# Output projections of 128 columns per column tile, all heads summed in PSUM, token rows copied by GpSimd, new part orders

## The chip, the cores and the metric

The kernel runs on one core of one Trainium2 chip. A core has TensorE (matrix multiplies into PSUM), VectorE, ScalarE and GpSimd (elementwise work; GpSimd here only on SBUF), and SyncE, which issues most of the DMAs. Each runs its own stream of instructions; semaphores tie them together. The metric is the device time in microseconds of one execution, median of three runs.

## The reference

The reference is one transformer layer on 2048 tokens of width 512. Part A is attention in 64 segments of 32 tokens with a recurrent memory of 8 rows: each segment attends, with 32 heads of 128, over 8 memory rows and its own 32 rows, and the first 8 rows of its output become the memory of the next segment. Part B is an MLP of width 1792 over all tokens. Cut to what matters:

```python
for s in range(n_seg):                       # 64 segments of 32 tokens
    xs = x[:, s * seg_len:(s + 1) * seg_len, :]
    h = jnp.concatenate([mem, xs], axis=1)   # 8 + 32 rows
    q, k, v = (jnp.einsum('btd,dhe->bhte', h, W) for W in (Wq, Wk, Wv))
    scores = jnp.where(mask, jnp.einsum('bhqe,bhke->bhqk', q, k) * scale, -1e9)
    o = jnp.einsum('bhqk,bhke->bhqe', softmax(scores), v)
    o = jnp.einsum('bhte,hed->btd', o, Wo)   # the output projection, sum over 32 heads
    mem = o[:, :M, :]
    outs.append(o[:, M:, :])
h = x + concatenate(outs)                    # x went in normalised
h2 = h + mlp(layernorm(h))                   # second norm inside mlp
```

## The kernel before

**Tiling.** A segment's tokens are split: 24 of its rows (`NA`) are packed with the 8 memory rows into one group of 32 (pack A), and the remaining 8 rows of four segments form another group of 32 (pack B). 32 columns are one column tile of TensorE, so most matmuls carry 32 columns of weights and four of them run side by side, at `tile_position` (0, 32 j). Each such matmul is issued with a weight load of its own. Where two steps in a row use the same activations as weights, the second drops its four loads (`matmul_kept`, line 547).

**A segment** (the loop over `s`, from line 1303) is a set of named parts. K0, K1, Q0, Q1, V0, V1 are passes of four units each (`passes`, matmuls on line 796, 512 columns of weights moving): a unit is four loads and four matmuls. SC0 and SC1 are scores (line 963), PV0, PV1 and PVA apply the probabilities to V (lines 994, 998, 1055), SA are the scores of the 24 + 8 rows (line 1025). F0 and F1 are passes of pack B for the next four segments in three segments out of four, and in the fourth one F1 is **WO_B** (`wo_B`), the output projection of pack B of the four segments before. **WO** (`wo`, `wo_units`) is the output projection of pack A, in eight units. Its result gives the memory rows of the next segment (tile hT) and 24 token rows of an earlier one (tile opT).

**WO before.** The heads are split into two halves by `a`, the 512 output columns into two halves by `b`; column tile j = 2a + b sums 16 heads into 256 columns of PSUM. Then VectorE transposes 128 x 256 (line 1095) into TT, and `halves_add` (line 1089) adds the two halves of heads, in two instructions for hT and two for opT. **WO_B before:** column tile j sums 8 heads into all 512 columns (line 1112); ScalarE copies half of it (line 1118), VectorE adds twice (lines 1119, 1120) into oBn, 32 rows by 512.

**`nat`** (line 1122) turns four segments' opT by a DMA transpose into oN, writes oBn's rows into oN by four DMAs, adds oN to the residual xr and takes the statistics of the second norm.

**What sets the order.** TensorE's order is written out by hand: `ORDERS` has for each kind of segment (`a1` to `a3` the first ones, `m0` to `m3` by s mod 4, `z60` to `z63` the last) a list of part.from.to; `TURNED` tells which passes run their four units backwards. The other engines are put in order by a list scheduler (`Sched.schedule`): a cost for each operation, a rank by the longest way to the end, plus `BONUS`, a table of numbers by kind and place. `S.either` lets it choose between ScalarE and VectorE. `align` adds weight loads that do nothing (line 794) to the passes: `LEAD` = 199 of them in all early on, and with `LOCK` = 106 up to a full count of 256 (`FETCH_N`) instructions every four segments, so that every four segments begin at the same place modulo 256. What follows the last segment (from line 1478) is the second half of part B, with 128-row matmuls.

Of the kernel before, what the change touches and what calls it, by code (L numbers as in the profile page):

```python
# [21 lines left out]
TURN = 1.27  # L22
# [4 lines left out]
LOCK = 106  # L27
# [9 lines left out]
BONUS = {"": 3.88, "EC0": 19.37, "EC0@a1": -40, "EC0@a2": 0, "EC0@a3": 2.13, "EC0@m0": 4.48, "EC0@m1": 40, "EC0@m2": 0, "EC0@m3": -7.71,  # L37
# [527 lines left out]
def build_kernel(nc, A_x, A_mem0, A_Wq, A_Wk, A_Wv, A_Wo, B_w1, B_b1, B_w2, B_b2, out):  # L565
# [3 lines left out]
    with st:  # L569
# [132 lines left out]
        def load(fn, kb, writes):  # L702
            chain.append(S.dma(fn, kb, writes=writes))
# [896 lines left out]
```

## Time and profile before

| | |
|---|---|
| device time, three runs | 804.42, 807.74, 809.25 us |
| median | 807.74 us |
| span of the profiled execution | 802.2 us |
| granted TensorE clock, mean | 0.998 |
| ScalarE busy | 558.0 us |
| GpSimd busy | 90.1 us |
| DMA moved | 48.77 MB, mean 61 GB/s |

The profile is one execution; its times are compared with its own span, which is 5.5 us below the median of the runs. In groups of instructions a row reads: line, engine, operation, what is written from what, shape, count, busy us in all, mean ns of one, and after the bar the engine's idle time just ahead of them with what ended it. In windows, each engine has its busy us and in brackets its instructions in the stretch, then the granted clock, the DMA share and GB/s. PEld is TensorE's weight loads. "issue" is time in which an engine waited for nothing that the profile shows. q8 is one of the DMA queues, of kind "instruction". A line can be a helper's, as 796 and 814 are.

### The profile page before, as it was taken

Reading aid. Unit: us, or ns where it says so; the run is one execution under the profiler, and the core shown is the slowest. Engines: PE = TensorE matmul, PEld = TensorE weight load, DVE = VectorE, ACT = ScalarE, POOL = GpSimd, SP = SyncE. Lnnn points to the kernel's source line nnn. Section 1 sums busy time; section 2 is a strip of 40 time slices with the busy share of each in tenths; the row PEclk is TensorE's granted clock in tenths of the full one; section 3 lists DMA queues with packets and bytes.
Section 4 is the critical chain, followed back from the end, with each engine's and each line's share of the span. In section 5 each row is a group of like instructions: output and inputs, shape, how many; then the busy total and the mean of one; then the engine's idle time right before and its main releaser. Section 6 shows DMA issues by size and latency. Waiting matters only on the chain.

```text
span 802.2 us, 46835 instructions
## 1 busy us (share of the span) xinstructions
PE 775.9 (97%) x21699; PEld 423.1 (53%) x20880; DVE 600.7 (75%) x1847; ACT 558.0 (70%) x1580; POOL 90.1 (11%) x211
## 2 busy tenths in 40 slices
PE   2899999999999999999999999999999999999998
PEld 1455555555555555555555555555555555644444
DVE  3277878888888888888888888888888888732311
ACT  1557777777777777777778777777777777773342
POOL 5022000010001010101010101000000000020700
PEclk9999999999999999999999999999999999999999
DMA  9961010201111121102010202010212112074300
GB/s 367 394 174 24 4 37 11 45 12 37 26 33 30 30 33 27 36 19 42 19 43 15 49 12 50 13 37 20 50 25 56 51 38 59 17 232 127 86 27 26
DMA packets 65555, 48.77 MB, mean 61 GB/s; under 512 B 28996, under 2 KB 63308, under 8 KB 63820
## 3 DMA queue, kind: packets, MB, share of 16 engines
q1 hardware_dynamic: 65024, 45.50, 20.3%
q8 instruction: 166, 2.72, 1.4%
q14 instruction: 33, 0.27, 0.1%
q10 hardware_dynamic: 332, 0.27, 0.1%
HBM read 31.08 MB, written 8.13 MB: 49 GB/s over the span
## 4 chain that ended last, share of the span: by engine, by line
PE 91%; DMA 3%; DVE 2%; ACT 1%; SPq 1%; issue 1%; POOL 0%; DVEq 0%; ACTq 0%
PE ps L796 43%; PE ps L1083 15%; PE ps L547 8%; PE quad L1465 6%; PE ps L1451 5%; DMA WQ<-in_A_Wq_dram 3%; PE ps L1112 3%; PE quad L994 3%; PE quad L1055 2%; PE ps L1025 2%; PE ps L1233 1%; PE ps L963 1%; PE quad L963 1%; SPq L708 1%; PE quad L998 1%
## 5 line engine op out<-in xcount | busy, mean ns | idle before, releaser
L1083 PE MATMUL ps<-WO,OT 128*32 128x256 bf16 x4224 | 140.6, 274 | 0.1
L796 PE MATMUL ps<-WQ,hT 128*32 128x512 bf16 x1864 | 131.6, 379 | 0.7 <-DVE hT L1089 0.5
L796 PE MATMUL ps<-WV,hT 128*32 128x512 bf16 x1364 | 125.2, 381 | 0.0
L796 PE MATMUL ps<-WK,hT 128*32 128x512 bf16 x1700 | 123.6, 380 | 0.1
L815 ACT ACTIVATE kq<-ps 128x512 bf16<-128x512 f32 x160 | 95.4, 597 | 32.3 <-PE ps L796 26.4
L1083 PEld LDWEIGHTS ps<-WO,OT 128*32 128x32 bf16 x4224 | 100.9, 96 | 26.5 <-ACT OT L814 5.5
L814 ACT CAST kq<-ps 128x512 bf16<-128x512 f32 x162 | 94.8, 585 | 19.9 <-PE ps L796 13.1
L814 ACT CAST OT<-quad 128x128 bf16<-128x128 f32 x191 | 84.4, 442 | 27.0 <-PE quad L998 18.8
L839 DVE STREAM_TRANSPOSE KALL<-kq 128x256 f32<-128x256 f32 x160 | 71.2, 445 | 15.0 <-ACT kq L814 11.8
L796 PEld LDWEIGHTS ps<-WQ,hT 128*32 128x32 bf16 x1864 | 50.3, 97 | 58.8 <-issue 19.0
L861 POOL COPY ZC<-QTB 128x256 bf16<-128x256 bf16 x64 | 25.6, 401 | 477.2 <-PE ps L963 455.7
L796 PEld LDWEIGHTS ps<-WK,hT 128*32 128x32 bf16 x1700 | 45.8, 96 | 56.9 <-issue 14.5
L547 PE MATMUL ps<-WV,hT 128*32 128x512 bf16 x684 | 67.6, 379 | 0.0
L796 PEld LDWEIGHTS ps<-WV,hT 128*32 128x32 bf16 x1364 | 38.4, 97 | 47.3 <-issue 36.6
L839 DVE STREAM_TRANSPOSE QT<-kq 128x256 f32<-128x256 f32 x128 | 57.0, 445 | 6.5 <-ACT kq L815 1.9
L1454 ACT ACTIVATE WQ<-ps,b1t 128x512 bf16<-128x512 f32 x42 | 28.9, 688 | 46.6 <-PE ps L1451 46.6
L1095 DVE STREAM_TRANSPOSE TT<-ps 128x256 f32<-128x256 f32 x66 | 29.7, 450 | 36.3 <-PE ps L1083 36.1
L814 ACT CAST VS<-ps 128x512 bf16<-128x512 f32 x65 | 38.1, 586 | 26.6 <-PE ps L796 26.5
L814 DVE CAST VS<-ps 128x512 bf16<-128x512 f32 x63 | 41.8, 663 | 5.4 <-PE ps L796 5.4
L1541 DVE TENSOR_TENSOR WV<-quad,WV 128x512 bf16<-128x512 f32 (+1 forms) x16 | 10.5, 672 | 45.6 <-PE quad L1465 45.6
L982 DVE TENSOR_TENSOR PC<-EC,rsc 128x128 bf16<-128x128 f32 x128 | 39.7, 310 | 4.3
L1112 PE MATMUL ps<-WO,OTB 128*32 128x512 bf16 x512 | 42.1, 381 | 0.4 <-issue 0.2
(163 smaller groups left out, 1432.1 us busy)
## 6 DMA issues: line engine op xcount, KB each, us to landing
WV<-in_A_Wv_dram SPq DMA_DIRECT2D x4, 1024.0 KB, 8.5
WK<-in_A_Wk_dram SPq DMA_DIRECT2D x4, 1024.0 KB, 14.2
WQ<-in_A_Wq_dram SPq DMA_DIRECT2D x4, 1024.0 KB, 24.7
WO<-in_A_Wo_dram SPq DMA_DIRECT2D x8, 512.0 KB, 9.4
v_last<-VSB SPq DMA_DIRECT2D x60, 64.0 KB, 2.9
VBD<-v_last SPq DMA_DIRECT2D x60, 64.0 KB, 2.9
h_mid<-xr SPq DMA_DIRECT2D x16, 128.0 KB, 1.8
WK<-in_B_w_dram SPq DMA_DIRECT2D x4, 512.0 KB, 4.6
```

The source lines that it names most:

```text
L547: return e.add_instruction(mybir.InstMatmult(name="I-%d" % (4000000 + _kept[0]), engine=mybir.EngineType.PE, start_tensor_calc=start, stop ...
L796: ins = e.matmul(o, l, m, start=(k == 0), stop=(k == DC - 1), tile_position=(0, 32 * j), skip_group_check=True)
L814: return {"act": (lambda e: e.copy(out, src), t_act(n, ps_)), "dve": (lambda e: e.tensor_copy(out, src), 0.16 + 1.042e-3 * n * fast)}
L815: return {"act": (lambda e: e.mul(out, src, scale_), t_act(n, ps_)), "dve": (lambda e: e.tensor_scalar(out, src, scale_, None, ALU.mult), ...
L839: S.op("dve", lambda e: e.transpose(out, src), reads=[("kq", i)], writes=[key], dur=t_dve(256) + 0.02, after=after)
L982: S.op("dve", lambda e: e.tensor_tensor(PC[:, r].rearrange("p t a -> p a t"), EC[:, r], bc, ALU.mult), reads=[("EC", r), ("rsc", r)], writ ...
L1083: ins = e.matmul(ps[bank][32 * j:32 * j + 32, 0:256], lhs(slot(h)), wo_cols(h, b), start=(k == 0), stop=(k == 15), tile_position=(0, 32 * ...
L1095: S.op("dve", lambda e: e.transpose(tt.rearrange("p c q t -> p (c q t)"), ps[bank][:, 0:256]), reads=[("ps", bank)], writes=[("TT", par)], ...
L1112: ins = e.matmul(ps[bank][32 * j:32 * j + 32, :], OTB[:, bk % 2, slot(h), :], WO[:, h, :], start=(k == 0), stop=(k == 7), tile_position=(0 ...
L1451: ins = e.matmul(ps[bank][:, 0:SBT], W1[:, cc, fc * P:(fc + 1) * P], hnT_of(k)[:, cc, :], start=(cc == 0), stop=(cc == DC - 1))
L1454: S.op("act", lambda e: e.activation(gT[:, fc, :], ps[bank][:, 0:SBT], ACTF.Gelu_apprx_tanh, bias=b1t[:, fc:fc + 1], scale=1.0), reads=[(" ...
L1465: S.op("pe", lambda e: e.matmul(quad[:, t, :], lhs, W2[:, fc, :], **flags), reads=[("W2", part_of(fc))] + gT_keys(k, fc), writes=[("ps", t ...
```

## The change

WO gives each column tile 128 of the 512 output columns and lets it sum all 32 heads, so nothing is left to be added after it. VectorE's transpose is 128 x 128; the memory rows go to hT by one copy on ScalarE or VectorE, the token rows to opT by one copy on GpSimd. WO_B uses the same units on OTB; its transpose goes to TTB, and GpSimd copies it into the rows of opT that were zero before. So `nat` needs no oBn and no four DMAs, and the memset of opT goes. WO's weights are loaded in head order. `LOCK` is None. `ORDERS` and `BONUS` are new throughout; `TURNED`, the banks and everything else stay.

```diff
-LOCK = 106
+LOCK = None
...
-          "m0": "Q0.0.2 Q1.0.1 Q0.2.4 K0.0.4 Q1.1.4 K1.0.4 SC0.0.1 V0.0.1 V1.0.2 V0.1.2 V1.2.3 V0.2.4 SC1.0.1 V1.3.4 F0.0.1 PVA.0.2 PV0.0.1 F0.1.4 WO.0.2 PV1.0.1 WO.2.8 F1.0.4 SA.0.1",
-          "m1": "K0.0.1 Q0.0.2 K0.1.2 Q0.2.4 K0.2.3 Q1.0.1 K0.3.4 Q1.1.4 K1.0.4 SC0.0.1 V1.0.1 V0.0.2 V1.1.2 V0.2.3 V1.2.3 V0.3.4 SC1.0.1 V1.3.4 F0.0.1 PVA.0.2 PV0.0.1 F0.1.4 WO.0.2 PV1.0.1 WO.2.8 F1.0.3 SA.0.1 F1.3.4",
-          "m2": "K0.0.2 Q0.0.4 K0.2.4 Q1.0.4 K1.0.4 SC0.0.1 V1.0.1 V0.0.2 V1.1.2 V0.2.3 V1.2.3 V0.3.4 SC1.0.1 V1.3.4 F0.0.2 PVA.0.2 PV0.0.1 F0.2.4 WO.0.2 PV1.0.1 WO.2.8 SA.0.1 F1.0.4",
-          "m3": "K0.0.1 Q0.0.2 K0.1.2 Q0.2.4 K0.2.4 Q1.0.4 K1.0.4 SC0.0.1 V1.0.1 V0.0.1 V1.1.2 V0.1.3 V1.2.3 V0.3.4 SC1.0.1 F1.0.1 V1.3.4 PVA.0.2 PV0.0.1 F1.1.5 WO.0.1 PV1.0.1 WO.1.8 F1.5.7 SA.0.1 F1.7.8",
+          "m0": "Q0.0.4 K0.0.3 Q1.0.1 K0.3.4 Q1.1.4 K1.0.4 V0.0.1 SC0.0.1 V0.1.3 V1.0.1 V0.3.4 F0.0.1 V1.1.2 F0.1.2 SC1.0.1 V1.2.4 PVA.0.2 PV0.0.1 F1.0.1 F0.2.4 WO.0.2 PV1.0.1 WO.2.8 SA.0.1 F1.1.4",
+          "m1": "Q0.0.4 K0.0.1 K1.0.1 K0.1.4 Q1.0.4 K1.1.4 V1.0.1 SC0.0.1 V0.0.2 V1.1.2 V0.2.4 V1.2.3 SC1.0.1 F0.0.1 V1.3.4 F0.1.3 PVA.0.2 PV0.0.1 F1.0.1 F0.3.4 WO.0.1 PV1.0.1 WO.1.8 F1.1.3 SA.0.1 F1.3.4",
+          "m2": "K0.0.2 Q0.0.4 K0.2.4 K1.0.1 Q1.0.4 K1.1.4 V1.0.1 SC0.0.1 V0.0.4 V1.1.2 SC1.0.1 F0.0.1 V1.2.4 F0.1.2 PVA.0.2 PV0.0.1 F0.2.4 WO.0.1 PV1.0.1 WO.1.3 F1.0.1 WO.3.8 F1.1.2 SA.0.1 F1.2.4",
+          "m3": "Q0.0.4 K0.0.2 Q1.0.1 K1.0.1 K0.2.4 Q1.1.3 V1.0.1 Q1.3.4 K1.1.4 V1.1.2 SC0.0.1 V0.0.1 V1.2.3 V0.1.4 SC1.0.1 F1.0.2 V1.3.4 F1.2.3 PVA.0.2 PV0.0.1 F1.3.5 WO.0.2 PV1.0.1 WO.2.8 SA.0.1 F1.5.8",
...
-        def wo_cols(h, dh):
-            return WO[:, h, :].rearrange("p (b two e) -> p two b e", two=2, e=32)[:, dh]
+        def wo_cols(h, j):
+            return WO[:, h, :].rearrange("p (c g e) -> p g c e", g=4, e=32)[:, j]
...
                 def f(e, q=q):
-                    for k in (2 * q, 2 * q + 1):
-                        for a in range(2):
-
-                            h = (k // 8) * 16 + 8 * a + k % 8
-                            for b in range(2):
-                                j = 2 * a + b
-                                ins = e.matmul(ps[bank][32 * j:32 * j + 32, 0:256], lhs(slot(h)), wo_cols(h, b), start=(k == 0), stop=(k == 15),
-                                               tile_position=(0, 32 * j), skip_group_check=True)
+                    for h in range(4 * q, 4 * q + 4):
+                        for j in range(4):
+                            ins = e.matmul(ps[bank][32 * j:32 * j + 32, 0:P], lhs(slot(h)), wo_cols(h, j), start=(h == 0), stop=(h == H - 1),
+                                           tile_position=(0, 32 * j), skip_group_check=True)
                     return ins
...
-            S.op("dve", lambda e: e.transpose(tt.rearrange("p c q t -> p (c q t)"), ps[bank][:, 0:256]), reads=[("ps", bank)], writes=[("TT", par)], dur=t_dve(256) + 0.02)
+            S.op("dve", lambda e: e.transpose(tt.rearrange("p c t -> p (c t)"), ps[bank][:, 0:P]), reads=[("ps", bank)], writes=[("TT", par)], dur=t_dve(P) + 0.02)
             if mem:
                 sl = (s + 1) % RING
-                S.op("dve", lambda e: [halves_add(tt, q2, hT[64 * q2:64 * q2 + 64, sl, :, NA:SEG], slice(NA, SEG))(e) for q2 in range(2)][1],
-                     reads=[("TT", par)], writes=[("hTm", sl)], dur=0.4)
+                S.either({"act": (lambda e: e.copy(hT[:, sl, :, NA:SEG], tt[:, :, NA:SEG]), 0.25),
+                          "dve": (lambda e: e.tensor_copy(hT[:, sl, :, NA:SEG], tt[:, :, NA:SEG]), 0.17)}, reads=[("TT", par)], writes=[("hTm", sl)])
             if xrows:
...
-                S.op("dve", lambda e: [halves_add(tt, q2, o[64 * q2:64 * q2 + 64], slice(0, NA))(e) for q2 in range(2)][1],
-                     reads=[("TT", par)], writes=[("opA", (sx // 4) % 2, sx % 4)], dur=0.53)
+                S.op("pool", lambda e: e.tensor_copy(o, tt[:, :, 0:NA]), reads=[("TT", par)], writes=[("opA", (sx // 4) % 2, sx % 4)], dur=0.36)

         def wo_B(bk, bank):

-            for k in range(8):
...
+            wo_units(lambda sl: OTB[:, bk % 2, sl, :], lambda r: [("OTB", bk % 2, sg) for sg in range(4)], bank)
+            S.op("dve", lambda e: e.transpose(TTB[:].rearrange("p c t -> p (c t)"), ps[bank][:, 0:P]), reads=[("ps", bank)], writes=["TTB"], dur=t_dve(P) + 0.02)
+            o = opT[:, bk % 2].rearrange("p c (s t) -> p c s t", s=4)[:, :, :, NA:SEG]
+            S.op("pool", lambda e: e.tensor_copy(o, TTB[:].rearrange("p c (s t) -> p c s t", s=4)), reads=["TTB"], writes=[("opB", bk % 2)], dur=0.43)
...
-            for sg in range(4):
-                S.dma(lambda e, sg=sg: e.dma_start(rows[32 * sg + NA:32 * sg + SEG, :], oBn[8 * sg:8 * sg + 8, :]), 8, reads=["oBn", "oN"], writes=[("oNr", sg)], occ=0.62)
```

More of the change, by code (lines that the diff above doesn't have):

```diff
@@ L616, in build_kernel @@
         OTB = sb("OTB", [P, 2, H, 32])
-        TT = sb("TT", [P, 2, DC, 2, 32], F32)
-        oBn = sb("oBn", [32, D])
+        TT = sb("TT", [P, 2, DC, 32], F32)
+        TTB = sb("TTB", [P, DC, 32], F32)
         opT = sb("opT", [P, 2, DC, P])
@@ L694, in build_kernel @@
         S.op("dve", lambda e: e.memset(KALL[:], 0.0), writes=[("KA", p, r) for p in range(2) for r in range(2)] + [("KB", p, r) for p in range(2) for r in range(2)], dur=2.3)
-        S.op("pool", lambda e: e.memset(opT[:], 0.0), writes=["opT0"] + [("opA", i, k) for i in range(2) for k in range(4)], dur=1.0)
         S.op("dve", lambda e: e.memset(OT[:], 0.0), writes=[("OTm", p, r) for p in range(2) for r in range(2)] + [("OTx", p) for p in range(2)], dur=1.0)
@@ L718, in build_kernel @@
         load_w(WQ, wq_d, "WQ")
-        for g in range(4):
-            for a in range(2):
-                h0 = 16 * (g // 2) + 8 * a + 4 * (g % 2)
-                load(lambda e, h0=h0: e.dma_start(WO[:, h0:h0 + 4, :], wo_d[:, h0:h0 + 4, :]), 590, [("WO", g, a)])
+        for q in range(8):
+            load(lambda e, q=q: e.dma_start(WO[:, 4 * q:4 * q + 4, :], wo_d[:, 4 * q:4 * q + 4, :]), 590, [("WO", q)])
         for tb in (2, 3, 4):
@@ L1076, in f @@
                 def f(e, q=q):
[L1077 to L1089 removed]
+                    for h in range(4 * q, 4 * q + 4):
+                        for j in range(4):
+                            ins = e.matmul(ps[bank][32 * j:32 * j + 32, 0:P], lhs(slot(h)), wo_cols(h, j), start=(h == 0), stop=(h == H - 1),
+                                           tile_position=(0, 32 * j), skip_group_check=True)
+                    return ins
+                S.op("pe", f, reads=[("WO", q)] + reads(q // 4), writes=[("ps", bank)], dur=0.22, mode=MC, ni=32)
         def wo(s, bank, mem=True, xrows=True):
@@ L1102, in wo @@
                 o = opT[:, (sx // 4) % 2, :, 32 * (sx % 4):32 * (sx % 4) + NA]
-                S.op("dve", lambda e: [halves_add(tt, q2, o[64 * q2:64 * q2 + 64], slice(0, NA))(e) for q2 in range(2)][1],
-                     reads=[("TT", par)], writes=[("opA", (sx // 4) % 2, sx % 4)], dur=0.53)
+                S.op("pool", lambda e: e.tensor_copy(o, tt[:, :, 0:NA]), reads=[("TT", par)], writes=[("opA", (sx // 4) % 2, sx % 4)], dur=0.36)
         def wo_B(bk, bank):
-            for k in range(8):
-                def f(e, k=k):
-                    for j in range(4):
-                        h = 8 * j + k
-                        ins = e.matmul(ps[bank][32 * j:32 * j + 32, :], OTB[:, bk % 2, slot(h), :], WO[:, h, :], start=(k == 0), stop=(k == 7),
-                                       tile_position=(0, 32 * j), skip_group_check=True)
-                    return ins
-                S.op("pe", f, reads=[("WO", g, a) for g in range(4) for a in range(2)] + [("OTB", bk % 2, sg) for sg in range(4)], writes=[("ps", bank)], dur=0.216, mode=MC, ni=8)
@@ L1116, in wo_B @@
-            okeys = [("OTB", bk % 2, sg) for sg in range(4)]
-            part_sum = view(OTB, (bk % 2) * H * 32, [64, D], F32)
-            S.named(S.op("act", lambda e: e.copy(part_sum, ps[bank][64:128, :]), reads=[("ps", bank)], writes=okeys, dur=t_act(512)), "WBa")
-            S.named(S.op("dve", lambda e: e.tensor_tensor(part_sum, ps[bank][0:64, :], part_sum, ALU.add), reads=[("ps", bank)] + okeys, writes=okeys, dur=t_dve(512)), "WBd")
-            S.op("dve", lambda e: e.tensor_tensor(oBn[:], part_sum[0:32], part_sum[32:64], ALU.add), reads=okeys, writes=["oBn"], dur=t_dve(512)).alone = True
+            wo_units(lambda sl: OTB[:, bk % 2, sl, :], lambda r: [("OTB", bk % 2, sg) for sg in range(4)], bank)
@@ L1122, in nat @@
+            S.op("dve", lambda e: e.transpose(TTB[:].rearrange("p c t -> p (c t)"), ps[bank][:, 0:P]), reads=[("ps", bank)], writes=["TTB"], dur=t_dve(P) + 0.02)
+            o = opT[:, bk % 2].rearrange("p c (s t) -> p c s t", s=4)[:, :, :, NA:SEG]
+            S.op("pool", lambda e: e.tensor_copy(o, TTB[:].rearrange("p c (s t) -> p c s t", s=4)), reads=["TTB"], writes=[("opB", bk % 2)], dur=0.43)
         def nat(bk):
             S.dma(lambda e: e.dma_start_transpose(oN[:], opT[:, bk % 2].rearrange("p c t -> p (c t)")), 256,
-                  reads=[("opA", bk % 2, k) for k in range(4)] + ["opT0"], writes=["oN"], occ=TURN)
@@ L1126, in nat @@
-            rows = oN[:].rearrange("p c t -> p (c t)")
-            for sg in range(4):
-                S.dma(lambda e, sg=sg: e.dma_start(rows[32 * sg + NA:32 * sg + SEG, :], oBn[8 * sg:8 * sg + 8, :]), 8, reads=["oBn", "oN"], writes=[("oNr", sg)], occ=0.62)
+                  reads=[("opA", bk % 2, k) for k in range(4)] + [("opB", bk % 2)], writes=["oN"], occ=TURN)
             xs = xr[:, bk % XR, :]
-            S.op("dve", lambda e: e.tensor_tensor(xs, xs, oN[:].rearrange("p c t -> p (c t)"), ALU.add), reads=["oN", ("xr", bk % XR)] + [("oNr", k) for k in range(4)],
+            S.op("dve", lambda e: e.tensor_tensor(xs, xs, oN[:].rearrange("p c t -> p (c t)"), ALU.add), reads=["oN", ("xr", bk % XR)],
```

9 lines of the change are left out of this document (2 added, 7 removed), and 151 rows, old and new, of tables (BONUS, ORDERS).

## The prediction

> **What bounds the kernel now.** I read the page first: how full TensorE is and how many instructions it takes.
>
> ```profile
> span 802.2 us, 46835 instructions
> PE 775.9 (97%) x21699; PEld 423.1 (53%) x20880; DVE 600.7 (75%) x1847; ACT 558.0 (70%) x1580; POOL 90.1 (11%) x211
> ...
> q8 instruction: 166, 2.72, 1.4%
> ```
>
> TensorE is busy 97%, VectorE 75%. 21699 + 20880 = 42579 TensorE instructions (matmuls and weight loads), and 166 packets of 2.72 MB / 166 = 16 KB on the instruction queue q8: 256 instructions of 64 bytes each. So q8 carries TensorE's program, packet by packet, while it runs. Next, ten periods of four segments as one stretch, with q8's line for the same stretch, and four short stretches.
>
> ```profile
> core 0: us, PE busy (x) PEld busy (x) DVE busy (x) ACT busy (x) POOL busy (x), PEclk, DMA share, GB/s
> 120.49:534.50 414.01, 412.69 (x13122) 228.44 (x12428) 359.22 (x1128) 316.96 (x940) 37.77 (x96) 1.00 0.14 30
> ...
> 159.12:162.94 3.82, 3.82 (x127) 2.67 (x128) 1.92 (x6) 2.25 (x6) 0.79 (x2) 1.00 0.15 43
> 427.65:431.17 3.52, 3.52 (x156) 2.47 (x142) 3.11 (x10) 2.85 (x10) 0.00 (x0) 1.00 0.13 42
> ...
> 406.73:410.78 4.05, 3.91 (x155) 2.64 (x140) 2.91 (x9) 2.71 (x10) 0.79 (x2) 1.00 0.26 69
> ```
>
> ```profile
> q8 instruction: 100, 1.64, 1.7%
> ```
>
> 13122 + 12428 = 25550 instructions and exactly 100 packets in 414 us: ten packets and 41.40 us for four segments, **4.14 us for a packet** on average. What is the least a packet can take? The timeline of TensorE answers, where it stops in the middle of a part and nothing in the profile releases it ("issue"):
>
> ```profile
> 158.09 0.36 PE L1055 MATMUL quad<-PTA,VS 32*128 32x32 bf16 x30
> 159.12 0.19 PE L1055 MATMUL quad<-PTA,VS 32*128 32x32 bf16 x2 [0.67 <-issue]
> 159.25 0.27 PE L994 MATMUL quad<-PTC,VS 32*128 32x16 bf16 x16
> 159.35 0.21 PE L998 MATMUL quad<-PTC,VBD 32*128 32x64 bf16 x4
> 159.49 1.05 PE L1112 MATMUL ps<-WO,OTB 128*32 128x512 bf16 x16
> 160.36 0.39 PE L1083 MATMUL ps<-WO,OT 128*32 128x256 bf16 x8
> 160.69 0.26 PE L994 MATMUL quad<-PTC,VS 32*128 32x16 bf16 x16
> 160.80 0.20 PE L998 MATMUL quad<-PTC,VBD 32*128 32x64 bf16 x4
> 160.93 1.71 PE L1083 MATMUL ps<-WO,OT 128*32 128x256 bf16 x56
> 162.47 0.87 PE L1112 MATMUL ps<-WO,OTB 128*32 128x512 bf16 x8
> ...
> 162.94 0.10 PEld L1112 LDWEIGHTS ps<-WO,OTB 128*32 128x32 bf16 x2 [0.38 <-issue]
> ```
>
> ```profile
> PEld ps L1112 <- issue: 4.9, 12, 0.7
> ...
> PEld quad L1055 <- issue: 7.1, 16, 0.8
> ```
>
> At 159.12 two matmuls of a group of 32 start 0.67 us late; at 162.94 two weight loads of a group of eight do. The window between holds 127 + 128 = 255 instructions: one packet. Both stops are at packet ends, and the stretch 406.73 to 410.78 ends in a third one (its window also counts instructions already under way at its edges, as that of 427.65 does). So **where a packet's instructions run out sooner, TensorE waits until about 3.82 us after the packet began.** The packet itself is short: 1.7% of 16 engines' 414 us, over 100, is 1.13 us, so most of the 3.82 us is latency of asking for the next packet only when one is begun. The list of waits shows twelve such stops in WO_B and sixteen in PVA, where instructions are dense; they cost little today, because 4.14 is above 3.82. The kernel sits 8% above its fetch floor.
>
> **The rule against this reading.** The Trainium skill, "Runtime: NRT & Kernel Launch", section "Instruction fetch mechanics", says that the program comes in 16 KiB blocks of 256 instructions and that the next block is fetched while the current one runs, so that crossing a block is mostly hidden. The block size agrees with q8; "mostly hidden" holds only while a block lasts longer than the stops above show. By that sentence the change would cost nothing in fetch; that outcome is the second rival.
>
> **The change, part by part.** First the matmuls of the two projections, with their weight loads.
>
> ```profile
> L1083 PE MATMUL ps<-WO,OT 128*32 128x256 bf16 x4224 | 140.6, 274 | 0.1
> L1083 PEld LDWEIGHTS ps<-WO,OT 128*32 128x32 bf16 x4224 | 100.9, 96 | 26.5 <-ACT OT L814 5.5 <-DVE rsc L979 1.3 <-issue 0.8
> L1112 PE MATMUL ps<-WO,OTB 128*32 128x512 bf16 x512 | 42.1, 381 | 0.4 <-issue 0.2
> ```
>
> *Instructions.* WO runs 66 times: 4224 / 66 = 64 matmuls and 64 loads; it becomes 32 heads x 4 column tiles = 128 and 128. So 128 instructions become 256. WO_B runs 16 times: 512 / 16 = 32 and 32 become 128 and 128, 64 become 256. The part orders hold 21 steps per four segments that reuse the weights of the step before (four loads saved each); the new ones, with the same directions, hold 8, which adds 13 x 4 = 52. LOCK = None drops the padding loads, about 20 per four segments (parts sum to 2540, ten packets are 2560). Four segments: 2560 + 4 x 128 + 192 + 52 - 20 = **3296, or 12.9 packets in place of 10**. Over segments 1 to 63, with their own orders, I count 51,536: 201.3 packets.
>
> *Streaming.* Four column tiles run side by side. 56 matmuls of 256 columns start over 160.93 to 162.47: 1.54 us / 14 rounds = 110 ns a round. Twice as many rounds of half the columns come to the same, if a 128-column round takes about 55 ns. The nearest shorter one:
>
> ```profile
> 404.23 0.30 PE L963 MATMUL quad<-KALL,ZC 128*32 128x64 bf16 x16
> 404.35 0.39 PE L796 MATMUL ps<-WV,hT 128*32 128x512 bf16 x4
> ```
>
> Sixteen matmuls of 64 columns, each with its load, take 0.12 us: 30 ns a round. Between 30 and 110 I take 55, so streaming costs nothing either way. WO_B: 32 x 55 = 1.76 us against 0.87 us / 4 x 8 = 1.74.
>
> *Fetch paces the segments.* 201.3 x 3.82 = 769 us; 63 segments take 63 / 4 x 41.40 = 652 us today: **+117 us**. Nothing hides this: TensorE has no other work while its program is missing. To that comes time in which the fetch rests. A segment's Q, K and V passes, 24 units of 0.22 us (0.87 / 4, WO_B's units above are of that size), hold with the scores about one packet; a packet wholly inside lasts some 5.4 us, 1.6 us above 3.82, and then the fetch idles. Each instruction by which a boundary lies off the start of that stretch swaps some 21 ns (5.4 us / 256) for 7 ns (1.76 us / 256 in WO), so the idling ends at 114 off; boundaries drift over 0 to 128, mean 1.6 x 114 / 2 / 128 = 0.7 us. Instructions queued ahead of the engine take part of it back. Between 0 and 0.7 us I take the middle, 0.35 x 63 = **+22 us** (0 to 44). Outside the segments three WO and one WO_B add 576 instructions, 2.25 packets or 8.6 us at most; loads from memory and long matmuls lie beside them: **+4** (0 to 9).
>
> *The copies.* What VectorE, ScalarE and the DMA queue lose or gain:
>
> ```profile
> L1089 DVE TENSOR_TENSOR opT<-TT 64x96 bf16<-64x96 f32 x128 | 32.6, 255 | 2.9
> L1095 DVE STREAM_TRANSPOSE TT<-ps 128x256 f32<-128x256 f32 x66 | 29.7, 450 | 36.3 <-PE ps L1083 36.1
> L1089 DVE TENSOR_TENSOR hT<-TT 64x32 bf16<-64x32 f32 x126 | 23.7, 188 | 3.0
> L1044 DVE STREAM_TRANSPOSE PTA<-PA 128x128 f32<-128x128 f32 x64 | 17.5, 273 | 0.1
> L1119 DVE TENSOR_TENSOR OTB<-ps,OTB 64x512 f32<-64x512 f32 x16 | 10.8, 675 | 4.4 <-ACT OTB L1118 4.4
> L1120 DVE TENSOR_TENSOR oBn<-OTB 32x512 bf16<-32x512 f32 x16 | 10.9, 679 | 0.3
> L757 POOL COPY hB<-xT 128x128 bf16<-128x128 bf16 x14 | 4.2, 301 | 5.3 <-DMA xT<-xn 5.3
> L796 PE MATMUL ps<-WQ,hT 128*32 128x512 bf16 x1864 | 131.6, 379 | 0.7 <-DVE hT L1089 0.5
> ```
>
> VectorE loses 32.6 + 23.7 + 10.8 + 10.9 us of adds, and 66 transposes fall from 450 to about 273 ns (12 us); it gains 16 of 273 ns (4 us): 74 us less, before the new copies into hT, at most 63 x 0.19 = 12. The recurrence WO, transpose, hT, next segment gets shorter, 450 + 2 x 188 against 273 + 188 ns, but TensorE lost only 0.7 us before those matmuls: worth at most that. GpSimd gets 80 copies of about 0.3 to 0.5 us, 40 us at most on an engine busy 11%. They wait there for a transpose at a segment's end; queued behind are the fills of ZC, which only the next scores need, and the small norm steps. SyncE loses 64 transfers of 8 KB into oN, none of which ends a wait of TensorE. All this is zero while TensorE waits for its program.
>
> *Sum* against the profiled execution: 802.2 + 117 + 22 + 4 = 945. The median run is 807.7, 5.5 above that span; a device time of **951 us**. The ends: at 3.52 us a packet, 708.6 - 652 = +57 with nothing beside it, 865; at 4.05 us, +163 + 44 + 9 = +216, 1024.
>
> **Rivals.**
> 1. *The clock falls as well.* Dense stretches leave TensorE working perhaps half of the time. In the opening the clock was halved after such a stretch:
>
> ```profile
> 39.00:40.00 1.00, 0.39 (x28) 0.27 (x32) 0.56 (x3) 0.61 (x3) 0.74 (x2) 1.00 1.12 354
> ...
> 41.00:42.00 1.00, 0.26 (x24) 0.19 (x20) 0.90 (x5) 1.00 (x5) 0.00 (x0) 1.00 1.10 352
> ...
> 43.00:44.00 1.00, 1.00 (x52) 0.94 (x48) 0.57 (x2) 0.61 (x2) 0.00 (x0) 0.50 1.10 347
> ```
>
> A passes stretch of 1.7 us that falls on half clock loses 0.9 us; once a segment that is 57 us: 1008. Against it: a slower TensorE also waits less. Chance 0.05 beyond the forecast.
> 2. *Not slower: the fetch keeps two packets under way when asked.* The point at which this decides is 41.40 / 12.9 = 3.2 us a packet: if packets can come faster than that, they are hidden in the mean. Then streaming is even, the stops now seen (4.9 + 7.1 us on the load side) and the 0.7 us before Q may go, some -5 us, and the time is about 803. For it: the packet itself lasts only 1.13 us. Against it: 255 instructions between two stops that are 3.82 us apart, with the second packet not there. Chance 0.07.
> 3. *Weight loads pace the rounds.* If a tile's next load cannot run under its own matmul, a round takes a load's 96 ns: 32 x 96 = 3.07 us, +1.32 for each WO and +1.34 for each WO_B, 66 and 16 times: +109, or 917. Against it stand the 30 ns rounds above, loads included. Chance 0.03. The Trainium skill's "TensorE: Matmul & The Clock Gate", section "Back-to-back issue gap", gives about 81 ns for a 128-column matmul in a stream of load and matmul pairs; by that figure, as an estimate, a WO takes 32 x 81 = 2.6 us; the 64-column rows here speak against it.
> 4. *Partly hidden*: the new orders spread the dense parts so that the fetch seldom waits; 815 to 878. For it: V steps now stand ahead of the scores. Against it: WO alone is one full packet in 1.76 us. Chance 0.05.
>
> **How the numbers follow.** Forecast 0.80, of which 0.75 between 878 and 1005 (periods of about 3.55 to 4.0 us); with rival 3 and a little of rivals 1 and 4 the range 878 to 1005 holds 0.8. A measurement of this kernel can tell about 0.5% from no change; faster by more: 0.03, half of rival 2's; within it 0.04; slower 0.93.
>
> **What would show it.** About 54,000 TensorE instructions and 210 packets on q8; stretches of 256 instructions 3.6 to 4.0 us apart in WO and WO_B with the idle time put down to issue; four segments in about 50 us; VectorE's busy time some 60 to 75 us lower with no gain from it. Wrong it would be if stops at packet ends stay below half a microsecond per segment, or if a 128-column round takes over 60 ns with its instructions at hand.

## The result, and the profile after

The changed kernel takes 964.96 us (median of four runs, 957.01 to 971.92) against 807.39 us for the kernel before on the same chip: a ratio of 1.192, 95% interval 1.186 to 1.198. It is slower by 157.6 us; 951 us were forecast, in a range of 878 to 1005. The ratio leaves out the slowest of the four executions (device time 971.92 us, over 1.5% above the fastest), and that one is the one profiled (span 970.1 us, mean granted clock 0.980), so its span lies 5 us above the median and not below it as before.

The page of the changed kernel: the span, the engines' busy time, the instruction queue, and the shares of the chain that ended last.

```profile
span 970.1 us, 58544 instructions
...
PE 807.9 (83%) x27441; PEld 490.9 (51%) x27138; DVE 515.0 (53%) x1570; ACT 575.1 (59%) x1634; POOL 111.1 (11%) x290
...
q8 instruction: 213, 3.49, 1.5%
...
PE 82%; issue 14%; DMA 1%; ACT 1%; DVE 1%; POOL 1%; ACTq 0%; DVEq 0%; POOLq 0%
```

The shares of the chain before:

```profile
PE 91%; DMA 3%; DVE 2%; ACT 1%; SPq 1%; issue 1%; POOL 0%; DVEq 0%; ACTq 0%
```

TensorE's share of the span fell from 97% to 83%, and the other engines did not fill the gap: VectorE and ScalarE are less full than before, GpSimd at 11% as full. The item that grew is "issue", from 1% to 14% of the chain. TensorE has 27441 + 27138 = 54,579 instructions, in 213 packets. The list of waits of the changed kernel (engine, tile, line, what it waited for: us in total, times, longest) says where:

```profile
PE ps L1074 <- issue: 70.1, 56, 2.2
...
PE ps L1020 <- issue: 27.8, 19, 2.2
...
PE ps L791 <- issue: 23.1, 25, 1.9
```

All of TensorE's idle time ahead of matmuls (rows PE; the loads, which overlap them, have rows of their own) that is put down to issue adds up to 131.6 us in this list, against 1.1 us in that of before; line 1074 is WO and WO_B, 1020 is SA, which comes right behind them. TensorE's waits for ScalarE and VectorE together are 5.9 us, against 6.2.

The same thirteen periods of four segments, from segment 8 to the end of segment 59, in the windows of the two kernels and with q8 over each. Before:

```profile
120.50:658.13 537.63, 536.26 (x17060) 297.42 (x16158) 464.99 (x1462) 412.01 (x1222) 44.96 (x114) 1.00 0.14 32
```

```profile
q8 instruction: 130, 2.13, 1.7%
```

After; the second, third and fourth rows are stretches from one stop that is put down to issue to a later one (the stop at 530.75 is one of 0.16 us ahead of a weight load), and the last two lie behind the fourth:

```profile
134.20:808.77 674.57, 566.97 (x21649) 356.89 (x21223) 395.30 (x1240) 426.10 (x1261) 62.92 (x179) 0.98 0.11 26
...
522.43:534.50 12.07, 10.57 (x389) 6.40 (x380) 7.68 (x23) 8.22 (x25) 0.67 (x2) 1.00 0.08 16
530.75:534.50 3.75, 2.25 (x131) 1.81 (x129) 0.98 (x2) 1.71 (x4) 0.00 (x0) 1.00 0.19 39
592.84:596.86 4.02, 2.04 (x129) 1.72 (x129) 0.00 (x0) 2.25 (x6) 0.00 (x0) 1.00 0.16 37
...
598.00:601.00 3.00, 2.42 (x116) 2.11 (x111) 1.19 (x4) 0.63 (x2) 0.27 (x1) 0.59 0.03 8
601.00:605.00 4.00, 4.00 (x96) 1.81 (x80) 3.11 (x11) 2.54 (x5) 0.30 (x1) 1.00 0.16 37
```

```profile
q8 instruction: 168, 2.75, 1.7%
```

Four segments took 537.63 / 13 = 41.36 us; they take 674.57 / 13 = 51.89 us, in 168 / 13 = 12.92 packets: 4.02 us for a packet, where before it was 4.14 with ten packets; the stretch from 522.43, at full clock, holds 768 instructions or so in 12.07 us, the same 4.02 for each 256. So the packets did not get slower in the mean; there are more of them. Carried over to 63 segments the difference is 63 / 4 x 10.53 = 166 us, which is nearly the whole difference of the spans (167.9 us).

The stretch from 592.84 is one packet exactly, as the timeline of TensorE in the changed kernel shows (start, us, what, and in brackets the idle time just before):

```profile
531.21 0.63 PE L1074 MATMUL ps<-WO,OT 128*32 128x128 bf16 x32
531.66 0.39 PE L791 MATMUL ps<-WV,hB 128*32 128x512 bf16 x4
```

```profile
592.84 0.24 PE L989 MATMUL quad<-PTC,VS 32*128 32x16 bf16 x12 [0.77 <-issue]
592.92 0.21 PE L993 MATMUL quad<-PTC,VBD 32*128 32x64 bf16 x4
593.05 0.63 PE L1074 MATMUL ps<-WO,OTB 128*32 128x128 bf16 x32
593.51 0.62 PE L1074 MATMUL ps<-WO,OT 128*32 128x128 bf16 x32
594.07 0.27 PE L989 MATMUL quad<-PTC,VS 32*128 32x16 bf16 x16
594.18 0.20 PE L993 MATMUL quad<-PTC,VBD 32*128 32x64 bf16 x4
594.31 0.57 PE L1074 MATMUL ps<-WO,OT 128*32 128x128 bf16 x28
596.86 1.88 PE L1074 MATMUL ps<-WO,OT 128*32 128x128 bf16 x68 [1.98 <-issue]
```

From one stop to the next stand 12 + 4 + 32 + 32 + 16 + 4 + 28 = 128 matmuls, each with its load: 256 instructions. They are done in about 2 us; then TensorE stands still for 1.98 us with its data ready, until 4.02 us after the packet began. The two rows of 531 give the price of a round: 32 matmuls start over 0.45 us, eight rounds of 56 ns. Behind the second stop the clock is halved for a while (0.59 in the row of 598).

The trace also records when each packet of q8 moves. The packet for which TensorE stood still before 596.86 began to move at 594.12, 1.28 us after the packet before it had begun to run; it landed at 595.53, and TensorE went on 1.33 us later. It is the same at all 88 stops of 0.3 us or more in the thirteen periods: each ends 1.18 to 1.60 us after a packet of q8 has landed, and together they are 106.0 of the 107.6 us in which TensorE stood idle there. No two packets overlap in time, and behind the 61 stops of 0.8 us or more the next packet began to move only 1.04 to 2.0 us after TensorE went on. So TensorE waits for its program, and the next packet begins to come only when the last one runs; when it is asked for, the trace does not say.

The groups that the change touches, in the changed kernel:

```profile
L1074 PE MATMUL ps<-WO,OT 128*32 128x128 bf16 x8448 | 160.3, 224 | 57.4 <-issue 56.5 <-ACT OT L809 0.2 <-DVE rsc L974 0.2
...
L1083 DVE STREAM_TRANSPOSE TT<-ps 128x128 f32<-128x128 f32 x66 | 20.9, 317 | 163.4 <-PE ps L1074 163.4
L1086 ACT CAST hT<-TT 128x32 bf16<-128x32 f32 x62 | 13.5, 218 | 70.8 <-DVE TT L1083 70.7
L1091 POOL CAST opT<-TT 128x96 bf16<-128x96 f32 x64 | 17.2, 269 | 305.2 <-DVE TT L1083 305.0
```

VectorE's busy time fell by 600.7 - 515.0 = 85.7 us, the adds and half of the transpose are gone, and the copies are small. None of it shortens the kernel.

### The profile page after: what moved, and what is told of

Read it like the earlier page. It is cut to its first block, busy times and chain, and to the rows that moved or that the text cites. A ratio compares the mean times of both kernels' runs of the same rounds, so it can differ in the third digit from the quotient of the medians.

```text
span 970.1 us, 58544 instructions
## 1 busy us (share of the span) xinstructions
PE 807.9 (83%) x27441; PEld 490.9 (51%) x27138; DVE 515.0 (53%) x1570; ACT 575.1 (59%) x1634; POOL 111.1 (11%) x290
## 4 chain that ended last, share of the span: by engine, by line
PE 82%; issue 14%; DMA 1%; ACT 1%; DVE 1%; POOL 1%; ACTq 0%; DVEq 0%; POOLq 0%
PE ps L791 42%; PE ps L1074 18%; PE quad L1440 5%; PE ps L1426 4%; PE ps L545 3%; PE quad L989 2%; PE quad L1050 2%; PE ps L1020 2%; PE ps L1208 1%; DMA xr<-in_A_x_dram 1%; PE quad L958 1%; PE ps L958 1%; PE quad L993 1%; PE ps L760 0%; POOL rst L731 0%
## 5 line engine op out<-in xcount | busy, mean ns | idle before, releaser
L1074 PE MATMUL ps<-WO,OT 128*32 128x128 bf16 x8448 | 160.3, 224 | 57.4 <-issue 56.5
L1074 PEld LDWEIGHTS ps<-WO,OT 128*32 128x32 bf16 x8448 | 129.9, 99 | 88.4 <-issue 69.5
L791 PE MATMUL ps<-WK,hT 128*32 128x512 bf16 x1864 | 143.8, 386 | 6.9 <-issue 6.9
L791 PE MATMUL ps<-WV,hT 128*32 128x512 bf16 x1852 | 139.1, 379 | 0.1
L809 ACT CAST OT<-quad 128x128 bf16<-128x128 f32 (+1 forms) x191 | 84.9, 445 | 53.9 <-PE quad L993 50.7
L1083 DVE STREAM_TRANSPOSE TT<-ps 128x128 f32<-128x128 f32 x66 | 20.9, 317 | 163.4 <-PE ps L1074 163.4
L809 ACT CAST VS<-ps 128x512 bf16<-128x512 f32 x111 | 64.9, 585 | 2.1 <-PE ps L791 1.1
L1074 PE MATMUL ps<-WO,OTB 128*32 128x128 bf16 x2048 | 43.8, 224 | 13.6 <-issue 13.5
L1020 PE MATMUL ps<-KALL,QT 128*32 128x32 bf16 x2048 | 30.4, 179 | 27.8 <-issue 27.8
L791 PE MATMUL ps<-WV,hB 128*32 128x512 bf16 x512 | 46.4, 394 | 4.0 <-issue 3.1
## 6 DMA issues: line engine op xcount, KB each, us to landing
WQ<-in_A_Wq_dram SPq DMA_DIRECT2D x4, 1024.0 KB, 25.7
```

The costliest lines, as they stand in the source:

```text
L791: ins = e.matmul(o, l, m, start=(k == 0), stop=(k == DC - 1), tile_position=(0, 32 * j), skip_group_check=True)
L809: return {"act": (lambda e: e.copy(out, src), t_act(n, ps_)), "dve": (lambda e: e.tensor_copy(out, src), 0.16 + 1.042e-3 * n * fast)}
L1020: ins = e.matmul(o[32 * j:32 * j + 32, 32 * k:32 * k + 32], QT[:, h // 2, :, h % 2], KALL[:, par * HP + h // 2, :, h % 2], start=False, st ...
L1074: ins = e.matmul(ps[bank][32 * j:32 * j + 32, 0:P], lhs(slot(h)), wo_cols(h, j), start=(h == 0), stop=(h == H - 1), tile_position=(0, 32 * ...
L1083: S.op("dve", lambda e: e.transpose(tt.rearrange("p c t -> p (c t)"), ps[bank][:, 0:P]), reads=[("ps", bank)], writes=[("TT", par)], dur=t ...
```

## The experiments

The theory is that the count of TensorE instructions, fetched 256 at a time, makes the loss. Three rivals were left by the result: the short rounds themselves; waits for data that come with the new copies, part orders or cost table; and the clock. The runs were made on three chips, each with its own runs of the kernel before (medians 805.16, 806.76 and 806.56 us), so they are compared by their ratios.

**The count without the narrow matmuls.** `x_padwo` keeps the old matmuls, orders and table and adds weight loads that do nothing: two before each matmul of WO, six before each of WO_B. That is the instruction count of the new projections in the same places. (`ni`, the instruction count that each operation gives the scheduler, is raised to match.)

```diff
-LOCK = 106
+LOCK = None
...
                             for b in range(2):
                                 j = 2 * a + b
+                                for _ in range(2):
+                                    e.ldweights(lhs(slot(h)), tile_position=(0, 32 * j))
...
+                        for _ in range(6):
+                            e.ldweights(OTB[:, bk % 2, slot(h), :], tile_position=(0, 32 * j))
```

> The kernel before, LOCK = None, with do-nothing weight loads: two more ahead of each matmul of WO, six more in WO_B, so that both hold 256 instructions as after the change; matmuls, rounds, copies, orders and results stay as before. Fetch theory: 3244 instructions in four segments, 12.7 packets x 3.82 = 48.4 us, 7.0 us above today's 41.4, times 15.75 = +110, and 0 to 44 of idle fetch: 915 to 960 us. Rival 'short rounds': no round is short here, 807 to 815 us. Rival 'order and copies': 807 us.

Measured: 951.99 us, ratio 1.1845 (1.1784 to 1.1907). Its windows and q8, thirteen periods:

```profile
133.26:789.70 656.44, 568.33 (x17061) 355.72 (x25116) 465.47 (x1462) 412.95 (x1222) 44.75 (x114) 0.99 0.11 27
```

```profile
q8 instruction: 165, 2.70, 1.7%
```

Matmuls, transposes, adds and copies are those of before; TensorE waits for issue 99.9 us in all. Loads alone make the kernel about as slow as the change does.

**The same count, spread out.** `x_spread6` adds six such loads to every unit of the passes instead, to the same 165 packets; `x_spread2` two, near the point where the packets' floor meets the old time.

```diff
-FETCH_AT, PADS, SLIP = 65, 8, 24
-LOCK = 106
+FETCH_AT, PADS, SLIP = 65, 6, 24
+LOCK = None
-LATE, RAW, LEAD = 0, 12, 199
+LATE, RAW, LEAD = 0, 12, 10**9
```

(`x_spread2` has PADS = 2.)

> The kernel before with six do-nothing weight loads in every unit of every pass (LEAD without end, PADS = 6, LOCK = None): 120 units x 6 = 720 more instructions in four segments, as many as the change adds, but spread over the long matmuls, where TensorE's loads have time. Fetch theory: 3260 instructions, 12.7 packets x 3.82 = 48.6 us, +7.2 x 15.75 = +113, little idle fetch: 905 to 930 us. Rival 'dense parts' (it is the number of instructions in a short time that TensorE cannot issue, not the fetch of packets): 807 to 820 us. Rivals 'short rounds' and 'order and copies': 807 us.

> The kernel before with two do-nothing loads in every pass unit, LOCK = None: 2540 + 240 = 2780 instructions in four segments, 10.9 packets x 3.82 = 41.5 us against 41.4 of work, the point at which fetch and work are even. Fetch theory: a few us more than before, 808 to 825 us, where six loads a unit gave 911; an extra load that cost by itself would give a third of that gain, 842 us.

Measured: 910.8 us, 1.1313 (1.1259 to 1.1367), and 826.64 us, 1.0247 (1.0228 to 1.0267). The windows and q8 of `x_spread6`:

```profile
135.87:760.66 624.79, 567.05 (x17060) 397.92 (x25324) 466.67 (x1462) 414.30 (x1222) 44.95 (x114) 1.00 0.12 28
```

```profile
q8 instruction: 165, 2.70, 1.9%
```

624.79 / 165 = **3.79 us a packet**, at full clock, with loads that TensorE could run beside its matmuls. This is the floor by itself, or just above it (3.82 was taken); it is a mean, for single packets began 3.27 to 4.87 us apart. Of the 87 us that the stretch grew by, 56 are TensorE's idle time (624.79 - 567.05 against 537.63 - 536.26); 31 are longer busy time. `y_bonus_only` below has as much, with no loads added and other stops (566.90 us), which speaks for the stops; but eleven stretches of half clock lie in its thirteen periods and none in these, so this is not shown, and a part may be the loads' own time. Against `x_padwo`, with the same count in one place, it is 41 us less: dense stretches cost more than the count, because the fetch rests while slow packets run (in `x_padwo` 44 of the 164 distances between the starts of packets are over 4.2 us, the longest 6.87; in `x_spread6` 13 of 164, the longest 4.87). `x_spread2` shows that the floor is not a sharp corner: 141 packets x 3.79 = 534 us would lie under the old 537.63, but the thirteen periods took 559.35 us, and the time came out just above the 808 to 825 us expected.

**The new matmuls, all short rounds, with fewer loads.** `x_kept` is the changed kernel in which three heads out of four use the weights of the first without a load. The new rounds, copies, orders and table stay; the projections then sum other products than the layer's, so this kernel measures time only. (`ni` is lowered to match.)

```diff
-                            ins = e.matmul(ps[bank][32 * j:32 * j + 32, 0:P], lhs(slot(h)), wo_cols(h, j), start=(h == 0), stop=(h == H - 1),
-                                           tile_position=(0, 32 * j), skip_group_check=True)
+                            if h % 4 == 0:
+                                ins = e.matmul(ps[bank][32 * j:32 * j + 32, 0:P], lhs(slot(h)), wo_cols(h, j), start=(h == 0), stop=(h == H - 1),
+                                               tile_position=(0, 32 * j), skip_group_check=True)
+                            else:
+                                ins = matmul_kept(e, ps[bank][32 * j:32 * j + 32, 0:P], lhs(slot(h - h % 4)), wo_cols(h, j), False, h == H - 1, (0, 32 * j), (P, 32))
```

> The kernel after, with the weight loads of three heads in four left out in both projections (their matmuls use the loaded head's weights, so the projections sum other products): all 128-column rounds, orders, copies and the cost table stay, and a projection holds 160 instructions in place of 256. Fetch theory: 2816 instructions in four segments, 11.0 packets x 3.82 = 42.0 us against 41.4, +10, and up to 30 for segments that hold two projections: 815 to 855 us, and the idle time put down to issue falls from 132 us to under 30. Rival 'order' (the new orders alone gave 945 us by waits for VectorE and ScalarE, and the missing instructions only hide these waits): above 900 us, with some 100 us of waits for these engines. Rival 'short rounds': 965 us if the matmuls, 820 to 900 us if the loads pace the rounds.

Measured: 841.44 us, 1.0431 (1.0405 to 1.0456).

```profile
124.43:691.07 566.64, 544.86 (x21647) 284.94 (x14980) 394.86 (x1240) 424.45 (x1261) 62.49 (x179) 1.00 0.12 30
```

The matmuls of the changed kernel are all there (21647 records against 21649), and with a quarter of the projections' loads nearly four fifths of the loss are gone (ratio 1.043 in place of 1.192). At most the 4.3% that are left can be the price of the short rounds, the copies and the new orders, and TensorE still waits 28.8 us for issue in it; q8 moved 144 packets in this stretch, 3.94 us each.

**The parts.** `x_wo` is the changed kernel with the old `ORDERS` and `BONUS`. `x_wo_only` changes WO alone in the kernel before, `x_wob_only` WO_B alone (both with `LOCK = None` and the copies that belong to the part).

```diff
-BONUS = {...}
-ORDERS = {...}
+BONUS = {...}
+ORDERS = {...}
```

> The new projections, copies and LOCK = None, with ORDERS and BONUS of before. Fetch theory: 3244 instructions in four segments, 12.7 packets as in the run with do-nothing loads in the projections, so the same 940 to 965 us, nearly all of the idle time put down to issue. Rival 'order': the old orders take most of the loss away, under 900 us.

> The kernel before with the new WO alone (WO_B, nat, ORDERS and BONUS as before, LOCK = None). Fetch theory: 3052 instructions in four segments, 11.9 packets x 3.82 = 45.5 us, +4.1 x 15.75 = +65, and some 10 to 35 for idle fetch: 875 to 910 us. Rival 'short rounds' at 96 ns a round: +87, 895 us. Rival 'order and copies': under 830 us, since the orders are the old ones.

> The kernel before with the new WO_B alone (with its transpose, GpSimd copy and nat), LOCK = None, ORDERS and BONUS of before. Fetch theory: 2732 instructions in four segments, 10.7 packets, 40.8 us in the mean, under the 41.4 of work; but the fourth segment holds WO and WO_B, 128 + 256 instructions, close together, so 815 to 845 us. If only the mean counted: 807 to 812 us. Rival 'short rounds' at 96 ns: +22, 829 us.

Measured: 964.8 us, 1.1937 (1.1862 to 1.2011); 931.88 us, 1.159 (1.1543 to 1.1637); 843.25 us, 1.0463 (1.0426 to 1.0501). The three longest waits of TensorE in `x_wo`:

```profile
PE ps L1076 <- issue: 79.7, 63, 3.3
PE ps L1022 <- issue: 18.1, 13, 1.9
PE ps L793 <- issue: 18.0, 18, 2.3
```

So the new orders and table together change nothing measurable in the changed kernel. With them the kernel has 12.92 packets where `x_wo` has 12.69, and waits 5.9 us for data where it waits 12.1. WO_B alone gives 10.69 packets for four segments, 40.5 us at the floor and so under the old 41.36, and yet costs 4.6% (0.7 of them for `LOCK = None`, as `y_nolock` below shows): of its 33.4 us of waits for issue 10.0 lie ahead of WO_B's matmuls and 8.5 ahead of WO's, so TensorE stops in the dense stretch whatever the mean is. `x_wo_only` came out above its expectation, 11.92 packets x 3.79 = 45.2 us against 49.50 measured for four segments. It has 82.0 us of issue and also 25.7 us of waits for ScalarE and VectorE, over 13 more than `x_padwo` and `x_wo` and nearly 20 more than the kernel before; which of the two takes the rest was not settled.

**The new orders and table in the old kernel.** `x_orders` gives the kernel before the new `BONUS` and `ORDERS`, `y_bonus_only` the new `BONUS` alone, `y_nolock` neither, only `LOCK = None`, which the other two have as well. The first shows what the new orders and table cost by themselves.

```diff
-LOCK = 106
+LOCK = None
-BONUS = {...}
+BONUS = {...}
```

(`y_bonus_only`; in `x_orders` ORDERS too, in `y_nolock` only the first pair.)

> The kernel before with the new ORDERS and BONUS and LOCK = None; both projections as before. Fetch theory (a packet of 256 TensorE instructions takes at least about 3.8 us, and the change needs 12.9 of them in four segments): here four segments hold 2592 instructions, 10.1 packets, 38.7 us against 41.4 of work, so 805 to 825 us. Rival 'order and copies' (the new orders, the cost table and the copies on other engines cost the time): most of the 157 us shows, above 870 us. Rival 'short rounds' (128-column rounds are paced by weight loads): 807 us.

> The kernel before with the new BONUS alone (old ORDERS, old projections, LOCK = None). The run with ORDERS and BONUS gave 945 us with waits for VectorE and ScalarE in place of issue. If the table does it (it lets VectorE and ScalarE take work in an order that suits the new, shorter copies and not the old adds): above 870 us, with the same kind of waits. If the part orders do it: under 830 us. Fetch theory says nothing on this: 9.9 packets are no bound.

> The kernel before with LOCK = None alone. 2540 instructions in four segments, 9.9 packets, below the work: the padding only chooses where packets end, so some stops move. Fetch theory: within about 1% of before, 803 to 815 us. It is the control for the runs that dropped the padding.

Measured: 945.08 us, 1.1738 (1.1705 to 1.1771); 963.43 us, 1.1943 (1.1918 to 1.1968); 810.95 us, 1.0066 (1.0046 to 1.0085). The expectation of `x_orders` failed by over 100 us. TensorE's waits in `y_bonus_only`:

```profile
PE quad L1053 <- DVE PTA L1042: 33.2, 14, 2.4
PE quad L961 <- ACT ZC L851: 27.9, 16, 1.9
PE ps L794 <- DVE hT L1087: 22.1, 17, 2.2
PE quad L1053 <- ACT EC L974: 21.3, 16, 1.5
```

This is another loss of the same size with another cause. Next to nothing waits for its program (3.7 us of issue), and of the 68 stops of 0.3 us or more in its thirteen periods only 8 end 1.1 to 1.7 us after a packet of q8 has landed; TensorE waits 124.7 us for VectorE and ScalarE, in the order that this table gives the old operations. The four rows have 14 to 17 waits each, about one in every four segments. In the changed kernel and in `x_kept` the same table goes with 5.9 and 4.7 us of such waits, so there this loss is absent; nothing in these runs ties the two sizes to each other. `y_nolock` prices the lost alignment: 5 us, with 8.1 us of issue against 1.1.

**Fewer instructions by other orders.** `y_reuse` is the changed kernel with the units of Q0 and Q1, K0 and K1, V0 and V1 taking turns in m0 to m3, so that 56 steps in four segments reuse their weights and only 3104 instructions are left; `TURNED` follows. `y_reuse_before` is the same in the kernel before, with `LOCK = None`. The cut shows m0 of `y_reuse`.

```diff
...
-          "m0": "Q0.0.4 K0.0.3 Q1.0.1 K0.3.4 Q1.1.4 K1.0.4 V0.0.1 SC0.0.1 V0.1.3 V1.0.1 V0.3.4 F0.0.1 V1.1.2 F0.1.2 SC1.0.1 V1.2.4 PVA.0.2 PV0.0.1 F1.0.1 F0.2.4 WO.0.2 PV1.0.1 WO.2.8 SA.0.1 F1.1.4",
+          "m0": "Q0.0.1 Q1.0.1 Q0.1.2 Q1.1.2 Q0.2.3 Q1.2.3 Q0.3.4 Q1.3.4 K0.0.1 K1.0.1 K0.1.2 K1.1.2 K0.2.3 K1.2.3 K0.3.4 K1.3.4 V1.0.1 V0.0.1 V1.1.2 V0.1.2 V1.2.3 V0.2.3 SC0.0.1 V1.3.4 V0.3.4 SC1.0.1 F0.0.1 F0.1.2 PVA.0.2 PV0.0.1 F1.0.1 F0.2.4 WO.0.2 PV1.0.1 WO.2.8 SA.0.1 F1.1.4",
...
```

> The kernel after, with the m0 to m3 orders rewritten so that Q0 and Q1, K0 and K1, V1 and V0 take turns unit by unit with the same weights (TURNED to match): 56 steps in four segments reuse weights, not 8, which takes 192 loads out; all work and results stay. 3104 instructions, 12.1 packets. Fetch theory: 0.8 packets or 2.9 us less in four segments, x 14 = -40, 915 to 940 us, if the later end of Q0 and K0 costs nothing of its own. Rivals 'order' and 'short rounds': 965 us or slower, since no round gets longer and the passes end later.

> The same rewrite of the m0 to m3 orders on the kernel before (LOCK = None, its own BONUS): 2400 instructions in four segments, 9.4 packets, 35.6 us against 41.4. Fetch theory: the stops at packet ends go, worth at most some 5 us; work and waits set the time, so 800 to 812 us, or more where the passes' later ends hold up the scores.

Measured: 1028.49 us, 1.2757 (1.2733 to 1.2781), and 898.12 us, 1.1143 (1.1117 to 1.1169). Both expectations failed. TensorE's waits in `y_reuse`:

```profile
PE ps L1074 <- issue: 59.0, 53, 2.0
PE quad L989 <- DVE PTC L978: 30.2, 56, 0.6
PE ps L1020 <- issue: 23.8, 17, 1.9
PE quad L1050 <- ACT EC L971: 22.5, 32, 1.4
```

The waits for issue fell from 131.6 to 94.1 us, about as much as the saved instructions should give; but those for VectorE and ScalarE rose from 5.9 to 79.2, and in `y_reuse_before`, where there is no fetch to save (5.8 us of issue), they are 74.4 us too. PV (line 989) now waits for its probabilities at nearly every segment (56 times), and PVA (line 1050) for ScalarE 32 times. That taking turns finishes both halves late and their copies then queue up would explain it, but was not tested. With 55.94 us for 158 / 13 = 12.15 packets, 4.60 us each, program and data now take turns in setting the pace.

All of it in one table, for thirteen periods of four segments of each profiled execution; "issue" and "data" are TensorE's waits ahead of matmuls over the whole execution, those put down to issue and those for ScalarE or VectorE, us.

| kernel | us, four segments | packets | us a packet | issue | data | ratio |
|---|---|---|---|---|---|---|
| before | 41.36 | 10.00 | 4.14 | 1.1 | 6.2 | 1 |
| y_nolock | 42.12 | 10.00 | 4.21 | 8.1 | 6.5 | 1.007 |
| x_spread2 | 43.03 | 10.85 | 3.97 | 13.8 | 6.4 | 1.025 |
| x_kept | 43.59 | 11.08 | 3.94 | 28.8 | 4.7 | 1.043 |
| x_wob_only | 44.07 | 10.69 | 4.12 | 33.4 | 8.1 | 1.046 |
| x_spread6 | 48.06 | 12.69 | 3.79 | 68.9 | 6.2 | 1.131 |
| x_wo_only | 49.50 | 11.92 | 4.15 | 82.0 | 25.7 | 1.159 |
| x_padwo | 50.50 | 12.69 | 3.98 | 99.9 | 12.3 | 1.185 |
| after | 51.89 | 12.92 | 4.02 | 131.6 | 5.9 | 1.192 |
| x_wo | 51.70 | 12.69 | 4.07 | 126.9 | 12.1 | 1.194 |
| y_reuse_before | 47.80 | 9.38 | 5.09 | 5.8 | 74.4 | 1.114 |
| x_orders | 50.62 | 10.15 | 4.99 | 0.9 | 104.7 | 1.174 |
| y_bonus_only | 51.74 | 9.92 | 5.21 | 3.7 | 124.7 | 1.194 |
| y_reuse | 55.94 | 12.15 | 4.60 | 94.1 | 79.2 | 1.276 |

In the upper part time follows packets at 3.8 to 4.2 us each; the last four leave that line, and they are those with data waits. No kernel here is faster than the one before.

## Why the prediction was right, point by point

**Instructions and packets: right.** 3296 instructions or 12.9 packets in four segments were counted, 12.92 measured; 54,579 instructions and 213 packets in all, against about 54,000 and 210.

**The floor of a packet: right.** Taken 3.82 us, measured 3.79 in `x_spread6`. By it the segments gain 63 / 4 x (12.92 x 3.79 - 41.36) = 120 us, against 117 in the sum. That it fits so closely is partly luck: 3.82 was read off one stretch between two stops, and single packets in `x_spread6` began 3.27 to 4.87 us apart. `x_padwo` shows that the count does this without any change to the arithmetic, and `x_kept` that most of it goes when the loads go.

**Time in which the fetch rests: right in kind, too small.** This is the term that was mis-sized. 0.35 us a segment was taken, the middle of 0 to 0.7. In the changed kernel (51.89 - 12.92 x 3.79) / 4 = 0.73 us, in `x_padwo` (50.50 - 12.69 x 3.79) / 4 = 0.60: over 63 segments 46 us and 38 us where 22 stood in the sum. In the changed kernel 44 of the 167 distances between the starts of packets are over 4.2 us, the longest 6.59, against 13 of 164 in `x_spread6`. That instructions queued ahead take part of the idle time back was the reason for the middle, and it did not show. This term, some 24 us too low in the profiled execution, is more than the 14 us by which the median was missed; that execution is 7 us slower than the median.

**Rival 1, the clock: it happened, small.** Apart from its very end, the clock in the trace of the changed kernel has eleven stretches of half speed, 3.4 us each, one of them that around 598 above; the first lies in the opening, where the kernel before has its only one. Nine lie in the thirteen periods. They are part of the 0.73 us just named and not on top of it: in the ten others than the first, 3.4 us each at half speed, at most some 17 us of work can be lost, and `x_padwo`, with only two of them in the thirteen periods, is 0.13 us a segment or 8 us lower.

**Outside the segments: right.** 4 us were taken; 167.9 - 120 - 46 = 2 us are left.

**Streaming: right.** A 128-column round takes 56 ns, 55 were taken. Rival 3, rounds paced by weight loads at 96 ns, falls by this.

**Rival 2, two packets under way: falls.** It needed packets 3.2 us apart or less; the least mean in any run is 3.79, and `x_spread6`, where the instructions lie evenly, is where it would have shown. The trace has it directly: in no run do two packets of q8 overlap, and no two start less than 3.23 us apart. So the sentence of the Trainium skill, "Runtime: NRT & Kernel Launch", section "Instruction fetch mechanics", that crossing a block is mostly hidden does not hold here; a block was hidden only where its 256 instructions took longer than about 3.8 us, the mean of single ones that vary. Rival 4, new orders that hide part, falls as well: `x_wo` with the old orders is the same.

**The copies: worth nothing, right.** VectorE is 85.7 us less busy and the end is not moved. The prediction wrote 74 us for its terms before the copies into hT, but 78 of adds and 12 of transposes less 4 of new ones make 86; and 62 of the 63 copies went to ScalarE, so next to nothing came off.

**LOCK: mis-sized by 5 us.** It was counted as 20 instructions less. `y_nolock` shows that the alignment itself was worth 0.7%.

**What was not seen.** That the cost table could cost 157 us in a kernel whose operations it was not made for was in no step. It did no harm to the forecast, since the table fits the changed kernel. The new orders without the new table, and the old table in `x_kept`, were not tried.

## What to carry to other kernels

Count instructions beside matmul time: cutting a matmul's columns in half with four column tiles keeps the streaming time and doubles the matmuls and their weight loads, and here a stretch whose 256 TensorE instructions take less than about 3.8 us waited for its program, even where a packet had more time than that in the mean (4.12 us in `x_wob_only`). Idle time of TensorE that nothing releases, at distances of 256 instructions and each time ending a little over 1 us after a packet of the instruction queue has landed, is the sign; what helped here was to take instructions out of the dense part, as keeping weights for several matmuls does in `x_kept`, where the arithmetic allows it, and in part to spread them out (`x_spread6` is 41 us faster than `x_padwo`). A table of scheduling costs belongs to the operations it was made for: move it with them, and price it in its own run before blaming or crediting it.

## What the runs showed of the hardware beyond what was expected

- Weight loads that do nothing are not free where TensorE has time to spare for them: six in each unit of the passes cost 13%, and of the 87 us that they added to the thirteen periods 56 are TensorE's idle time.
- A packet is fetched late, not slowly: its transfer takes 1.7% of 16 engines' 674.57 us over 168, or 1.1 us, but it begins over 1 us after the packet before has begun to run, and TensorE goes on only 1.18 to 1.60 us after the landing; together that is about the 3.8 to 4.0 us from one packet to the next.
- The clock was halved for 3.4 us at a time though no stop for issue ahead of a matmul was longer than 2.2 us; in the stretch from 592.84, just ahead of one such time, it was busy 2.04 of 4.02 us.
